# Attention results in the rotating FFN banks, last output tile in three parts, and a new planned order, in a fused attention and maxout-FFN kernel

## The chip, the cores and the metric

One core of one Trainium2 chip. The metric is the device time of one execution in microseconds (us). Most executions of a kernel agree within 0.3%; only runs in the fast state are compared, unless it is said otherwise. The profile's span (first to last instruction) is some 1.8 us shorter than the time.

## The reference

```python
# q, k, v: (4, 8, 768, 64) fp32; n_global 8, n_local 96; w1, w2, w3: (512, 768); w_out: (768, 512)
scores = q @ k.T / sqrt(64) - slope[h] * dist          # ALiBi-like bias
keep   = (key < 8) | (0 <= row - key < 96)              # first 8 keys, and a window of 96
a      = softmax(where(keep, scores, -1e9))
x      = (a @ v), heads joined                          # 3072 tokens x 512
h      = max(x @ w1, x @ w2, x @ w3)
out    = h @ w_out                                      # 3072 x 512, fp32
```

The 3072 tokens are 24 tiles of 128. A tile attends to itself and the tile before it. The FFN runs on seven chunks of 4, 2, 2, 4, 4, 4, 4 tiles.

## The kernel before

All instructions are emitted from one list, the planned order. A unit such as `S12.0.0` is a letter (what), a tile or chunk, and choices (head group, engine). The letters that matter: `S` scores and exp, `M` mask, `A` results times v with normalisation, `T` transpose of a result tile (`.4`: by DMA), `X`, `x` transpose of q and k, `F c.f.j` FFN unit of chunk c, slice f, weight j, `O` output unit, `w g.j` load of FFN weight j (its first 256 columns for g 0, the other 512 for g 1), `W g.j` cast of the third number g of its 768 columns, `E` the last chunk's output. Where a last digit names an engine, 0 is ScalarE, 1 VectorE and 2 GpSimd. Each engine runs its share of the list strictly in order.

```python
xb_pool  = tile_pool(name="xb",  bufs=3)       # attention result of a tile, bf16
ost_pool = tile_pool(name="ost", bufs=4)       # output staging
psS = tile_pool(name="psS", bufs=1, space=PSUM)  # tags sp0, sp1: two banks each
psH = tile_pool(name="psH", bufs=3, space=PSUM)  # tag h: three banks in rotation
psT = tile_pool(name="psT", bufs=1, space=PSUM)  # tag tp: one bank
# ... cut ...
def u_A(T, g):                                  # results times v
    op = psS.tile([128, 4, 65], FP32, name="op", tag=f"sp{g}")   # reuses its scores' banks
    # ... 8 matmuls ...
    nc.vector.reciprocal(rz, op[:, :, 64])
    nc.vector.tensor_tensor(out=x[:, 4*g:4*g+4], in0=op[:, :, 0:64], in1=rz..., op=mult)   # x is xb[T]

def u_XT(T, how):
    if how == 4:
        nc.sync.dma_start_transpose(out=xT[c][...], in_=xb[T]...)
    # ... cut: else on TensorE ...

def u_F1(c, f, j):                              # 4 matmuls into an h bank, then
    # j == 0: ACT copies it; j == 1, 2: VectorE takes the maximum with what is there

def f2_out(po, c, tt, copy, cols=slice(0, DM)):
    ost = ost_pool.tile(list(po.shape), FP32, name="ost", tag="ost")
    copy(ost, po)
    nc.sync.dma_start(out=out[T * 128:(T + 1) * 128, cols], in_=ost)

def u_E():                                      # last chunk: tiles 0..2 as 512 columns, then
    for i, copy in enumerate((nc.scalar.copy, nc.vector.tensor_copy)):
        cols = slice(i * 256, (i + 1) * 256)    # tile 3 in two halves
        # ... 6 matmuls, copy, store ...
```

The softmax here doesn't subtract the row's maximum and nothing guards it: scores larger than these inputs give would overflow.

## Time and profile before

| | before |
|---|---|
| median of 6 runs, us | 182.34 (182.04 to 182.61) |
| span of the profiled run, us | 180.0 |
| TensorE, VectorE, ScalarE busy | 93%, 68%, 60% |
| first FFN matmul, end of the last matmul, us | 24.98, 176.7 (its start plus its 0.11; the chain, with modelled ends, has 176.88) |

A page of the profile gives busy time per engine, then 40 slices of the span with tenths of busy time. The chain of work that ended last is followed back from the end, so an interval that stands in it is one that the next step waited for. PE is TensorE, PEld its weight loads, DVE VectorE, ACT ScalarE, POOL GpSimd, SPq and ACTq the DMA issues of SP and ACT. The lines themselves stand in the prediction.

### The profile page before, as it was taken

To read this page: it belongs to the slowest core of one execution; us is meant where nothing else is said; L and a number is where in the kernel's file an instruction comes from. 1 tells how busy PE (TensorE), PEld (TensorE's weight loads), DVE (VectorE), ACT (ScalarE), POOL (GpSimd) and SP (SyncE) were. 2 spreads that over 40 slices of the span, in tenths; PEclk is the share of its full clock that TensorE was granted. 3 is DMA by queue.
4 is the path that set the end of the run, shared out by engine and by line. 5 is a ranking of instruction groups with operands and counts; after the bars stand their busy time and mean duration, and the time that the engine had idled before them with its cause. 6 is when DMAs were issued, how large, how long until landed. Compare 5 with 4: busy or idle time off the path is not lost.

```text
span 180.0 us, 4007 instructions
## 1 busy us (share of the span) xinstructions
PE 167.2 (93%) x1534; PEld 94.5 (52%) x1534; DVE 122.0 (68%) x282; ACT 108.2 (60%) x164; POOL 35.0 (19%) x59
## 2 busy tenths in 40 slices
PE   0589979999999999999999999999999999999993
PEld 0345645555876787665455454454444545444442
DVE  3446477688796788769889878778877755144620
ACT  4987894966988867688555536374271753322122
POOL 6423524522052224201032001111004000000000
PEclk9999999999999999999999999999999999999999
DMA  5999999999988999999999999995998434610006
GB/s 147 275 267 284 263 350 306 355 254 261 298 178 198 274 213 234 103 232 265 187 185 249 160 232 226 257 140 136 252 198 166 99 93 146 204 58 0 4 0 233
DMA packets 91251, 35.91 MB, mean 200 GB/s; under 512 B 76000, under 2 KB 85984, under 8 KB 91232
## 3 DMA queue, kind: packets, MB, share of 16 engines
q1 hardware_dynamic: 91232, 35.66, 91.2%
q8 instruction: 12, 0.20, 0.5%
q14 instruction: 7, 0.06, 0.1%
HBM read 25.17 MB, written 6.29 MB: 175 GB/s over the span
## 4 chain that ended last, share of the span: by engine, by line
PE 78%; DMA 9%; SPq 9%; POOL 2%; issue 1%; DVE 0%; DVEq 0%; POOLq 0%
PE h L336 50%; PE po L351 16%; PE sp L260 5%; SPq L163 4%; DMA wst<-in_moe_w_dram 4%; SPq L148 3%; DMA qkT<-qkb 3%; PE op L297 3%; DMA xT<-xb 2%; PE op L300 2%; PE tp L238 1%; SPq L392 1%; PE xtp L324 1%; POOL w L402 1%; POOL qkb L185 1%
## 5 line engine op out<-in xcount | busy, mean ns | idle before, releaser
L336 PE MATMUL h<-xT,w 128*128 128x512 bf16 (+1 forms) x504 | 101.4, 349 | 0.8 <-DMA xT<-xb 0.4
L336 PEld LDWEIGHTS <-w 128*128 128x128 bf16 x504 | 46.3, 98 | 40.5 <-POOL w L402 0.9
L265 ACT ACTIVATE P<-sp 128x1024 bf16<-128x1024 f32 (+1 forms) x48 | 43.3, 950 | 22.5 <-PE sp L260 22.5
L351 PE MATMUL po<-wo,ht 128*128 128x512 bf16 (+1 forms) x150 | 33.9, 371 | 0.0
L343 DVE TENSOR_TENSOR h<-h,h 128x512 bf16<-128x512 bf16 (+1 forms) x42 | 25.2, 608 | 12.8 <-PE h L336 12.0
L341 ACT CAST h<-h 128x512 bf16<-128x512 f32 (+1 forms) x42 | 21.6, 531 | 18.5 <-PE h L336 18.0
L284 DVE TENSOR_TENSOR P<-P,wmask 128x1024 bf16<-128x1024 bf16 x34 | 23.4, 693 | 9.0 <-ACT P L265 8.9
L345 DVE TENSOR_TENSOR ht<-h,h 128x512 bf16<-128x512 bf16 (+1 forms) x42 | 25.2, 608 | 3.3 <-PE h L336 2.6
L357 ACT COPY ost<-po 128x512 f32<-128x512 f32 (+1 forms) x21 | 12.0, 577 | 18.4 <-PE po L351 16.0
L351 PEld LDWEIGHTS <-ht 128*128 128x128 bf16 x150 | 14.0, 98 | 14.7
L307 DVE TENSOR_TENSOR xb<-op,rz 128x256 bf16<-128x256 f32 x48 | 20.4, 424 | 1.7
L260 PE MATMUL sp<-qkT 64*128 64x128 bf16 x352 | 15.1, 220 | 1.1 <-DVE qkT L221 0.9
L297 PEld LDWEIGHTS <-P 128*128 128x128 bf16 x192 | 13.7, 99 | 4.3 <-ACT P L265 1.2
L260 PEld LDWEIGHTS <-qkT 64*128 64x128 bf16 x352 | 9.9, 94 | 11.3 <-issue 6.6
L297 PE MATMUL op<-va,P 128*128 128x65 bf16 x160 | 14.0, 193 | 0.9 <-ACT P L265 0.8
L306 DVE RECIPROCAL rz<-op 128x4 f32<-128x4 f32 x48 | 8.5, 178 | 9.2 <-PE op L300 5.8
L218 PE MATMUL tpp<-identb,qkp 128*128 128x128 bf16 x64 | 6.2, 254 | 6.6 <-DVE qkp L170 6.6
L300 PEld LDWEIGHTS <-P 128*128 128x128 bf16 x160 | 10.8, 97 | 1.5
L300 PE MATMUL op<-va,P 128*128 128x65 bf16 x128 | 11.2, 193 | 0.0
L176 POOL CAST va<-rawv 128x512 bf16<-128x512 f32 x9 | 5.8, 644 | 17.2 <-PE h L336 9.4
L185 POOL CAST qkb<-raw 128x1024 bf16<-128x1024 f32 x5 | 5.2, 1038 | 19.1 <-issue 13.6
L202 POOL COPY va<-vaf 8x260 int32<-8x260 int32 x10 | 4.4, 440 | 22.5 <-PE op L300 22.5
(68 smaller groups left out, 116.0 us busy)
## 6 DMA issues: line engine op xcount, KB each, us to landing
rawv<-in_v_dram SPq DMA_DIRECT2D x24, 256.0 KB, 5.5
out_dram<-ost SPq DMA_DIRECT2D x23, 256.0 KB, 3.1
raw<-in_q_dram SPq DMA_DIRECT2D x16, 256.0 KB, 5.3
raw<-in_k_dram SPq DMA_DIRECT2D x16, 256.0 KB, 5.0
wst<-in_moe_w_dram SPq DMA_DIRECT2D x3, 1024.0 KB, 9.9
rawp<-in_q_dram SPq DMA_DIRECT2D x4, 512.0 KB, 6.6
rawp<-in_k_dram SPq DMA_DIRECT2D x4, 512.0 KB, 6.5
wst<-in_moe_w_dram SPq DMA_DIRECT2D x3, 512.0 KB, 6.6
```

The source lines that it names most:

```text
L260: nc.tensor.matmul(sp[:, hh, j2, ds], qT(T - ds, 1)[hsl, jp], qT(T, 0)[hsl, jp], start=not how, stop=True, skip_group_check=True)
L265: nc.scalar.activation(P[:, :, 0:n], sp.rearrange("p a b d n -> p (a b) d n")[:, :, 0:n], AF.Exp, bias=0.0, scale=scale)
L284: nc.vector.tensor_mul(P, P, wmask[:, g, :, 0:2])
L297: nc.tensor.matmul(o, P[:, i, 0], heads(va[T])[:, h], start=True, stop=(t == 0), skip_group_check=True)
L300: nc.tensor.matmul(o, P[:, i, 1], heads(va[T - 1])[:, h], start=False, stop=True, skip_group_check=True)
L307: nc.vector.tensor_tensor(out=x[:, 4 * g:4 * g + 4], in0=op[:, :, 0:64], in1=rz[:, :, None].to_broadcast([128, 4, D]), op=ALU.mult)
L336: nc.tensor.matmul(ps, w123[f // 2][:, dm, j, (f % 2) * 128:(f % 2) * 128 + 128], xT[c][:, dm], start=(dm == 0), stop=(dm == 3))
L341: nc.scalar.copy(h01, ps)
L343: nc.vector.tensor_max(h01s[c, f], h01s[c, f], ps)
L345: nc.vector.tensor_max(ht[c][:, f], h01s[c, f], ps)
L351: nc.tensor.matmul(po, ht[c][:, f, tt * 128:(tt + 1) * 128], wo[:, f, cols], start=(f == 0), stop=(f == NF - 1))
L357: copy(ost, po)
```

## The change

The intent is to free the score banks earlier, shorten the end, and use both in a better order.

```diff
-    def u_A(T, g):
+    def u_A(T, g, how):
-        op = psS.tile([128, 4, 65], FP32, name="op", tag=f"sp{g}")
+        pool, tag = (psH, "h") if how else (psS, f"sp{g}")
+        op = pool.tile([128, 4, 65], FP32, name="op", tag=tag)
 ...
-    def f2_out(po, c, tt, copy, cols=slice(0, DM)):
+    def f2_out(po, c, tt, copy, cols=slice(0, DM), dma=nc.sync):
-        nc.sync.dma_start(out=out[T * 128:(T + 1) * 128, cols], in_=ost)
+        dma.dma_start(out=out[T * 128:(T + 1) * 128, cols], in_=ost)
 ...
-        for i, copy in enumerate((nc.scalar.copy, nc.vector.tensor_copy)):
-            cols = slice(i * 256, (i + 1) * 256)
+        for lo, hi, copy, dma in ((0, 256, nc.scalar.copy, nc.sync), (256, 384, nc.vector.tensor_copy, nc.sync),
+                                  (384, 512, nc.scalar.copy, nc.scalar)):
 ... (the planned order: all 506 units in a new order, many casts and copies on another engine; 41 of 48 A units with how = 1; excerpt)
-    ... M5.1 W1.0.2 F0.2.0 F0.3.0 F0.4.0 c3.0.2 x3.0.3 ...
+    ... W1.0.0 l3.1 W2.0.0 w1.1 v4 F0.0.2 S5.0.0 S5.1.0 M5.0 M5.1 F0.2.0 F0.3.0 F0.1.2 F0.4.0 ...
-    ... C20.0.3 v20 C18.1.1 O3.0.1 S18.0.0 ... T17.4 F4.2.2 O3.2.0 A19.0 A19.1 T18.4 ...
+    ... O3.0.0 O3.1.1 C20.1.0 S19.0.0 X21.4 S19.1.0 A18.1.1 M19.0 O3.2.0 O3.3.0 X22.4 T17.4 A19.0.1 G19.2 T18.4 ...
```

More of the change, by code (lines that the diff above doesn't have):

```diff
@@ L25 @@
 SCHEDULE = """
-    K0 K1 K2 K3 K4 K5 K6 K7 l1.0 v0 v1 B0.1 B1.0 c0.0.1 c0.1.1 B2.1 B3.1 B4.2 B5.0 B6.0 x0.0.2 x0.1.3
-    c1.0.0 S0.0.1 B7.2 S0.1.1 M0.0 M0.1 C0.1.2 C1.1.0 A0.0 G0.0 x1.0.2 A0.1 S1.0.1 S1.1.1 l1.1 M1.0 G1.1
-    l2.0 c1.1.2 l2.1 M1.1 c2.0.1 v2 w0.1 v3 v4 x1.1.2 w0.0 A1.0 A1.1 c2.1.2 V1.2 x2.0.1 C2.1.2 S2.0.1
-    S2.1.1 G2.2 C3.1.2 T0.1 M2.0 M2.1 A2.0 x2.1.2 A2.1 V2.1 S3.0.1 S3.1.1 T1.0 T2.0 G3.2 W0.1.2 M3.0
-    M3.1 A3.0 W0.0.2 A3.1 S4.0.0 T3.1 w0.2 S4.1.0 M4.0 M4.1 G4.1 C4.1.1 W0.2.0 F0.0.0 V3.1 F0.1.0 F0.0.1
@@ L31 @@
-    w1.0 F0.1.1 A4.0 A4.1 F0.0.2 F0.1.2 W2.0.0 S5.0.0 M5.0 l3.0 S5.1.0 M5.1 W1.0.2 F0.2.0 F0.3.0 F0.4.0
-    c3.0.2 x3.0.3 v5 C5.1.2 T4.0 w1.1 V4.2 A5.0 W2.1.0 l3.1 F0.5.0 W1.1.2 c3.1.1 F0.2.1 F0.3.1 x3.1.2
-    A5.1 F0.4.1 w1.2 W1.2.0 F0.5.1 S6.0.0 S6.1.0 v6 C6.1.0 v7 C7.1.0 T5.0 M6.0 M6.1 W2.2.2 F0.2.2 F0.3.2
-    F0.4.2 F0.5.2 F1.0.0 F1.1.0 A6.0 F1.2.0 A6.1 L8 F1.0.1 F1.1.1 o2 Q2.0 G6.0 S7.0.0 o0 S7.1.0 F1.2.1
-    G7.0 F1.0.2 F1.1.2 T6.0 M7.0 M7.1 F1.3.0 F1.4.0 F1.5.0 A7.0 C8.0.2 X8.3 A7.1 Q0.0 v8 o1 L9 L10
@@ L36 @@
-    F1.3.1 F1.4.1 F1.5.1 S8.0.0 S8.1.0 v9 V7.2 G8.1 L11 C8.1.0 M8.0 Q1.2 O0.0.0 v10 v11 C9.0.2 M8.1
-    O0.1.0 A8.0 X9.0 A8.1 V8.2 O0.2.0 C10.0.0 T7.1 F1.2.2 F1.3.2 F1.4.2 S9.0.0 M9.0 S9.1.0 M9.1 C9.1.2
-    L12 L13 L14 G9.1 X10.1 O0.3.0 F2.0.0 F2.0.1 A9.0 F2.1.0 A9.1 F1.5.2 F2.0.2 v12 F2.2.0 T8.1 S10.0.0
-    S10.1.0 F2.1.1 F2.2.1 F2.3.0 C11.0.2 X11.0 M10.0 F2.4.0 M10.1 F2.1.2 F2.5.0 V9.2 G10.1 C10.1.2 A10.0
-    A10.1 V10.2 C11.1.2 C12.0.2 X12.4 C12.1.2 C13.0.0 X13.4 F2.2.2 T9.1 F2.3.1 F2.3.2 L15 S11.0.0 M11.0
@@ L41 @@
-    S11.1.0 v13 v14 v15 v16 M11.1 O1.0.0 F2.4.1 A11.0 O1.1.0 T10.0 A11.1 F2.5.1 F2.4.2 T11.0 S12.0.0
-    M12.0 S12.1.0 G12.1 M12.1 F2.5.2 C14.0.0 F3.0.0 F3.1.0 A12.0 A12.1 F3.0.1 C15.0.1 X14.3 S13.0.0
-    S13.1.0 G13.1 M13.0 M13.1 X15.4 O2.0.0 C13.1.0 F3.0.2 C14.1.1 C15.1.2 F3.2.0 A13.0 A13.1 C16.1.1
-    F3.1.1 F3.2.1 S14.0.0 S14.1.0 G14.2 V13.1 T12.4 M14.0 M14.1 F3.3.0 F3.1.2 F3.4.0 L16 T13.4 A14.0
-    A14.1 F3.3.1 F3.4.1 S15.0.0 S15.1.0 C16.0.3 L17 L18 M15.0 M15.1 F3.5.0 T14.4 O2.1.0 G15.2 V14.2
@@ L46 @@
-    A15.0 X16.1 A15.1 V15.2 T15.4 F3.2.2 F3.3.2 C17.0.0 F3.4.2 S16.0.0 M16.0 S16.1.0 L19 F3.5.1 F3.5.2
-    X17.4 v17 A16.0 M16.1 F4.0.0 F4.1.0 C18.0.3 F4.0.1 F4.1.1 G16.2 v18 C17.1.0 A16.1 F4.0.2 X18.4
-    F4.1.2 S17.0.0 S17.1.0 L20 T16.4 F4.2.0 F4.3.0 F4.4.0 V16.1 C19.0.1 M17.0 X19.4 L21 M17.1 v19 A17.0
-    A17.1 C20.0.3 v20 C18.1.1 O3.0.1 S18.0.0 M18.0 S18.1.0 O3.1.0 C19.1.2 M18.1 F4.2.1 A18.0 A18.1
-    F4.3.1 F4.4.1 G18.1 X20.4 S19.0.0 S19.1.0 C20.1.0 F4.5.0 M19.0 M19.1 T17.4 F4.2.2 O3.2.0 A19.0 A19.1
@@ L51 @@
-    T18.4 F4.5.1 T19.4 L22 V19.2 G19.2 C21.0.3 O3.3.1 S20.0.0 M20.0 S20.1.0 G20.1 X21.4 v21 L23 v22
-    F4.3.2 v23 F4.4.2 A20.0 F4.5.2 M20.1 F5.0.0 F5.0.1 F5.1.0 A20.1 C22.0.1 C23.0.2 F5.0.2 F5.1.1
-    S21.0.0 S21.1.0 F5.2.0 M21.0 M21.1 F5.3.0 F5.2.1 F5.3.1 C21.1.0 C22.1.2 F5.1.2 X22.4 O4.0.0 V20.1
-    A21.0 T20.4 A21.1 F5.2.2 F5.3.2 G21.0 S22.0.0 S22.1.0 M22.0 M22.1 F5.4.0 F5.4.1 X23.4 G22.1 C23.1.0
-    V21.2 A22.0 F5.5.0 A22.1 O4.1.0 F5.5.1 S23.0.0 M23.0 S23.1.0 F5.4.2 M23.1 T21.4 T22.4 O4.2.0 F5.5.2
@@ L56 @@
-    O4.3.0 V22.1 A23.0 A23.1 T23.4 O5.0.0 O5.1.0 O5.2.0 O5.3.1 F6.0.0 F6.1.0 F6.2.0 F6.0.1 F6.1.1 F6.2.1
-    F6.3.0 F6.0.2 F6.1.2 F6.2.2 F6.4.0 F6.5.0 F6.3.1 F6.4.1 F6.3.2 F6.4.2 F6.5.1 F6.5.2 E
+    c0.0.2 K0 B0.0 l1.0 K1 l1.1 l2.0 K2 K3 K4 B1.1 B2.0 B3.1 B4.0 B5.0 B6.0 x0.0.0 B7.0 c0.1.2 c1.0.2
+    c1.1.1 x0.1.2 x1.0.3 c2.0.1 S0.0.0 S0.1.1 G0.1 S1.0.0 v0 x1.1.1 v1 M0.0 K5 K6 K7 M0.1 M1.0 l2.1
+    C0.1.2 S1.1.1 M1.1 G1.2 S2.0.1 M2.0 v2 C1.1.1 v3 w0.0 w0.1 w0.2 A0.0.1 A0.1.1 S2.1.0 G2.2 c2.1.2
@@ new lines @@
+    x2.0.0 A1.0.1 S3.0.1 A1.1.1 C2.1.2 V1.2 M2.1 T0.0 M3.0 S3.1.1 C3.1.1 A2.0.1 A2.1.1 T1.0 V2.2 A3.0.0
+    x2.1.0 M3.1 T2.0 A3.1.0 T3.1 W0.0.2 G3.2 S4.0.0 S4.1.0 W0.2.1 M4.0 F0.0.0 F0.1.0 w1.0 V3.1 M4.1 l3.0
+    W0.1.2 F0.0.1 F0.1.1 G4.2 W1.0.0 l3.1 W2.0.0 w1.1 v4 F0.0.2 S5.0.0 S5.1.0 M5.0 M5.1 F0.2.0 F0.3.0
+    F0.1.2 F0.4.0 w1.2 c3.0.2 c3.1.2 x3.0.3 x3.1.0 W1.2.2 W1.1.1 W2.1.0 C4.1.1 F0.5.0 S6.0.1 S6.1.0 G6.2
+    W2.2.0 F0.2.1 F0.3.1 v5 A4.0.1 F0.4.1 F0.5.1 A4.1.1 o2 S7.0.0 V4.2 L8 S7.1.0 F0.2.2 T4.0 C5.1.2
@@ new lines @@
+    A5.0.1 A5.1.1 F0.3.2 F0.4.2 T5.0 F0.5.2 F1.0.0 v6 F1.0.1 C8.0.2 X8.3 M6.0 F1.1.0 F1.2.0 F1.3.0 M6.1
+    M7.0 C6.1.0 G7.0 L9 F1.1.1 F1.2.1 o0 F1.0.2 M7.1 F1.4.0 Q2.2 C9.0.2 X9.3 F1.3.1 F1.4.1 S8.0.0 S8.1.0
+    G8.1 L10 C10.0.2 A6.0.1 v7 F1.1.2 F1.2.2 o1 F1.5.0 F1.5.1 F1.3.2 F1.4.2 L11 v8 Q0.0 v9 C7.1.2 X10.0
+    A6.1.1 L12 S9.0.0 S9.1.0 A7.0.1 A7.1.1 Q1.2 F1.5.2 M8.0 C11.0.1 X11.4 L13 T6.0 v10 V7.2 O0.0.0
+    C8.1.0 O0.1.0 G9.1 S10.0.0 v11 M8.1 M9.0 S10.1.0 A8.0.1 A8.1.1 T7.1 T8.4 O0.2.0 O0.3.0 F2.0.0 M9.1
@@ new lines @@
+    M10.0 V8.2 F2.1.0 M10.1 C9.1.1 C12.0.1 F2.0.1 F2.0.2 G10.0 S11.0.0 S11.1.0 F2.1.1 A9.0.1 X12.1
+    F2.2.0 F2.3.0 A9.1.1 F2.1.2 C10.1.0 C13.0.2 X13.3 F2.4.0 S12.0.0 L14 V9.2 S12.1.0 A10.0.1 M11.0
+    M11.1 v12 v13 A10.1.1 V10.2 C11.1.1 O1.0.0 T9.0 M12.0 G12.0 O1.1.0 F2.2.1 F2.3.1 F2.5.0 v14 L15
+    C12.1.2 C13.1.2 T10.0 A11.0.1 A11.1.1 v15 v16 S13.0.0 S13.1.0 F2.2.2 F2.3.2 F2.4.1 F2.5.1 T11.1
+    G13.0 L16 F2.4.2 C14.0.0 C15.0.2 F2.5.2 A12.0.1 M12.1 M13.0 M13.1 X14.0 F3.0.0 F3.1.0 A12.1.1 F3.0.1
@@ new lines @@
+    F3.1.1 F3.2.0 A13.0.0 A13.1.0 F3.0.2 X15.4 F3.1.2 C14.1.1 C15.1.1 S14.0.0 S14.1.0 G14.2 V13.1 M14.0
+    M14.1 F3.3.0 C16.1.2 F3.4.0 C16.0.0 T12.4 T13.4 O2.0.1 A14.0.1 F3.2.1 F3.2.2 A14.1.1 S15.0.0 M15.0
+    S15.1.0 F3.5.0 X16.4 v17 T14.0 G15.0 V14.1 M15.1 L17 F3.3.1 F3.3.2 L18 v18 v19 F3.4.1 C17.1.0 F3.4.2
+    A15.0.1 A15.1.1 S16.0.0 M16.0 S16.1.0 G16.2 C17.0.1 F3.5.1 F3.5.2 T15.0 X17.4 O2.1.1 M16.1 C18.0.0
+    V15.2 F4.0.0 F4.1.0 A16.0.0 L19 F4.0.1 F4.1.1 A16.1.1 C18.1.2 S17.0.0 S17.1.0 M17.0 F4.0.2 F4.2.0
@@ new lines @@
+    F4.2.1 F4.1.2 M17.1 F4.3.0 C19.0.2 F4.3.1 F4.2.2 F4.3.2 L20 C20.0.0 V16.2 X18.4 S18.0.0 M18.0 T16.4
+    S18.1.0 L21 L22 F4.4.0 A17.0.1 F4.5.0 A17.1.1 F4.4.1 F4.5.1 F4.4.2 F4.5.2 G18.0 v20 C21.0.2 C22.0.3
+    C19.1.2 X19.4 X20.4 M18.1 A18.0.1 v21 O3.0.0 O3.1.1 C20.1.0 S19.0.0 X21.4 S19.1.0 A18.1.1 M19.0
+    O3.2.0 O3.3.0 X22.4 T17.4 A19.0.1 G19.2 T18.4 S20.0.0 S20.1.0 M19.1 M20.0 O4.0.1 A19.1.1 M20.1
+    C21.1.2 T19.4 L23 G20.2 S21.0.0 M21.0 v22 S21.1.0 V19.2 O4.1.0 G21.2 A20.0.1 O4.2.1 v23 S22.0.0
@@ new lines @@
+    S22.1.0 A20.1.1 O4.3.0 V20.1 A21.0.1 M21.1 M22.0 M22.1 G22.2 F5.0.0 F5.1.0 F5.0.1 F5.2.0 C23.0.1
+    F5.3.0 A21.1.1 F5.1.1 F5.0.2 C22.1.0 V21.2 A22.0.1 F5.2.1 X23.4 F5.1.2 T20.4 T21.4 F5.2.2 S23.0.0
+    S23.1.0 C23.1.1 A22.1.1 F5.4.0 M23.0 V22.2 M23.1 F5.5.0 A23.0.0 F5.3.1 A23.1.0 T22.4 T23.4 F5.4.1
+    F5.5.1 F5.3.2 F5.4.2 F5.5.2 F6.0.0 F6.0.1 O5.0.1 O5.1.0 F6.0.2 F6.1.0 F6.2.0 F6.3.0 F6.4.0 F6.1.1
+    F6.2.1 F6.3.1 F6.4.1 F6.1.2 F6.2.2 F6.3.2 O5.2.1 O5.3.1 F6.4.2 F6.5.0 F6.5.1 F6.5.2 E
@@ L376, in u_E @@
             f2_out(po, last, tt, nc.scalar.copy)
-        for i, copy in enumerate((nc.scalar.copy, nc.vector.tensor_copy)):
-            cols = slice(i * 256, (i + 1) * 256)
-            po = psH.tile([128, 256], FP32, name="po", tag="h")
-            f2_mm(po, last, n - 1, range(NF), cols)
-            f2_out(po, last, n - 1, copy, cols)
+        for lo, hi, copy, dma in ((0, 256, nc.scalar.copy, nc.sync), (256, 384, nc.vector.tensor_copy, nc.sync),
+                                  (384, 512, nc.scalar.copy, nc.scalar)):
+            po = psH.tile([128, hi - lo], FP32, name="po", tag="h")
+            f2_mm(po, last, n - 1, range(NF), slice(lo, hi))
+            f2_out(po, last, n - 1, copy, slice(lo, hi), dma)
     wsrc = [moe_w1, moe_w2, moe_w3]
```

## The prediction

> **What bounds the kernel now.** I read the page first. Section 1 and the tenths line of section 2 show TensorE (PE) busy for 93% of a span of 180.0 us, idle only in the first slices and the last (a slice is 4.5 us):
>
> ```profile
> span 180.0 us, 4007 instructions
> PE 167.2 (93%) x1534; PEld 94.5 (52%) x1534; DVE 122.0 (68%) x282; ACT 108.2 (60%) x164; POOL 35.0 (19%) x59
> PE   0589979999999999999999999999999999999993
> DVE  3446477688796788769889878778877755144620
> DMA  5999999999988999999999999995998434610006
> ```
>
> Busy PE is not proof of a dense PE, so I took a table of stretches (columns: stretch, length, then busy time and number of instructions per engine, clock, DMA share, GB/s) and the chain of work that ended last in order of time (start, length, what):
>
> ```profile
> 0.00:5.84 5.84, 0.00 (x0) 0.00 (x0) 2.23 (x14) 3.59 (x8) 4.12 (x14) 1.00 0.68 180
> 5.84:24.98 19.14, 16.03 (x208) 9.93 (x208) 10.49 (x27) 17.08 (x26) 7.70 (x11) 1.00 1.18 277
> 24.98:76.00 51.02, 51.02 (x550) 34.52 (x551) 40.24 (x95) 38.78 (x60) 15.11 (x19) 1.00 1.04 251
> 103.00:150.00 47.00, 47.00 (x386) 23.15 (x384) 36.01 (x79) 23.94 (x36) 4.50 (x8) 1.00 0.90 179
> ```
>
> ```profile
> 16.89 6.95 DMA wst<-in_moe_w_dram
> 23.83 0.05 issue
> 23.89 1.05 POOL w L402
> 24.94 0.05 issue
> 24.98 3.63 PE h L336 x16
> ...
> 97.12 4.38 DMA xT<-xb
> ...
> 150.95 5.18 PE po L351 x24
> 156.13 15.54 PE h L336 x72
> 171.67 5.21 PE po L351 x30
> 176.88 0.04 DVEq L357
> ...
> 176.96 0.42 DVE ost L357
> ```
>
> So there are three regions. **Head** (to 24.98): loads, casts, exp and masks of the first tiles; it ends when the first FFN weight has landed and been cast. **Body** (24.98 to 176.88): PE back to back; starts that came late behind a wait (read in the timeline) add up to about 1.1 us, the largest 0.6 at 101.5 (a transposing DMA of xb) and 0.4 at 76.5 (one of qkb). **Tail** (3.1 us): last copy, last store. The list of waits says the same: after the head the matmuls wait 0.4 us for xT by DMA and 0.2 for qkT by DMA, and nothing larger.
>
> **What the Trainium skill says.** "TensorE: Matmul & The Clock Gate", section "Wait — 56ns, not 53.3ns?": back-to-back 512-column matmuls start 215.7 ns apart when warm. The trace agrees: 24 in 5.18 us is 216 ns. "PSUM — Partial Sum Buffer", Specifications: 8 banks of 2 KiB per partition, a matmul output at most one. By the pools all are taken: sp0 and sp1 two each, three for h, one for tp. No spare bank exists, so results times v must borrow. "DMA: Bandwidth & Descriptors", "Issuing engines are not separate DMA queues": a second issuing engine saves only issue time; here an output store's issue takes 0.33 us. "ScalarE: Activation LUTs", "What ACT_TABLE_LOAD costs": an ACTIVATE with immediates takes 186 ns + 0.833 ns per column; the 512-column copies of this trace took 577 ns on average (formula 613), so 128 columns are estimated at 0.29 us.
>
> **The change part by part.**
> (1) 41 of the 48 results-times-v units write into a rotating h bank instead of the sp bank that their scores used. Removed: scores of the next tile waiting for VectorE to read op; they now wait only for the exp. Work stays the same. As the body has almost no waits, this itself can save at most part of 1.1 us there; it helps the head, where scores, exp, mask and results follow closely. Added: the h rotation of three is used 197 times instead of 159. A bank is reusable about 0.85 us after results times v (gap 0.2, RECIPROCAL 0.18, TENSOR_TENSOR 0.42), 0.8 to 0.9 after an FFN unit. I laid both orders out by PE work and looked three users back: before one place falls short, by 0.1 us; after four, 0.6 us together, if the readers are free.
> (2) PE work. Units: FFN 4x0.216=0.864 (two-tile chunks 4x0.109), output 6x0.216=1.296, results 8x0.03=0.24, scores 8x0.0275+0.12=0.33, bias 0.53 more, transposes 0.056 each. Without the final unit the old order sums to 157.6 and the new to 156.75: two fewer biased scores (8 to 6, and one moved to a half-size tile), one more xT transposed on PE (12 to 11 by DMA). The 0.85 saved lies in the head, where PE is not the limit.
> (3) Head. Weights w0 are loaded earlier: 4.5 MB (units of 1024 KB) ahead of and including the first weight instead of 5.25, so that it is no longer last to arrive. Walking the new order by hand: ten masks and biases on ACT at 0.44 end near 8.1, then two qkT copies (1.0 each), exp 0.97 each; the second tile pair's qkT is on VectorE at 15.1, exp of tile 3 ends at 21.3, its results are scaled at 22.8, transposed and copied at 23.6. The first FFN matmul comes at about **23.9** instead of 24.98.
> (4) What that is worth is decided later: the FFN's third weight w1.2 is the last to land. In the old trace casts began at 34.62 (w1.1, 8.5 MB of loads) and 39.11 (w1.2, 10.0 MB), and the first matmul with the latter at 40.69. In the new order w1.1 still has 8.5 MB, w1.2 9.75, as one v tile moved behind. 1.5 MB took 4.49 us, so w1.2 should land 0.75 us earlier, 38.35, and with POOL's cast of 1.04 be usable at **39.4**. PE gets there at 39.4 to 39.9: after 35.3 (w1.1 at 34.6 plus a VectorE cast of 0.69) come 4 FFN units, two results and two half scores, 4.6 us. From there remain 130.5 us of PE work after and 130.0 before, plus 5.2 of the final unit. Check on the old kernel: 40.69+130.0+5.2=175.9, and measured 176.88; the missing 1.0 is its waits. New: 39.4+130.5+5.2=175.1, plus waits.
> (5) Waits of the new body, the term I know least. Shortfalls of the h rotation 0.6; the last chunk's xT: between tile 23's results and its FFN stand five FFN units (4.3 us) where four outputs (5.2 us) stood, against about 1.3 on VectorE and 2.4 to 3.6 of DMA, about 0.2; VectorE, given more copies (output copies on it 3 to 8, v casts 4 to 8), is loaded to about 104% of PE time in one 10 us stretch near chunk 1, about 0.4. Sum **1.2**, end of PE 176.3, or 0.6 before the old.
> (6) Tail. 12 matmuls of 256 columns become 6 of 256 and 12 of 128: same PE time. The last copy goes from VectorE 0.42 to ACT about 0.29, which is reached some 0.1 later; the last store halves. SP was not behind (five issues of 0.33 to 0.41), so a second queue saves little. Gain **0.2**.
> Sum: -0.6 - 0.2 = -0.8, so 182.3 becomes **181.5 us**.
>
> **Rivals.** *Rotation becomes the bound*: each borrowed bank waits for VectorE, 68% busy on average and 77 to 79% in the long stretches of the body; if it is 0.15 us late at 20 places, waits are 3 us more and the time is 184. For it: VectorE is in order and its masks (0.69) stand before these reads. Against: the new order puts 3 to 15 us of PE work between scores and results where 2 to 6 stood. *Free PE*: looser spacing takes away all body waits and loads arrive sooner; then PE ends at 175.1 or slightly earlier, and the time is 180 to 180.3. Against a larger gain: the matmuls themselves do not shrink, and DMA is at full share until 45 us. *Head gain wholly lost*: the weights decide, landing as before; PE ends where it did, 182.1 to 182.5. *Transposing DMAs*: 11+10 instead of 12+10, in other places; if two come late, as at 76 and 101 before, +1.
>
> **Range and chances.** The head's arrival is uncertain by 0.7 us, waits by about +2 and -1, tail by 0.2: 180.0 to 183.6 eight times in ten. Faster by over 2% means under 178.7, below even the wait-free sum by 1.4, so 0.04. Slower means over 186.0, 4 us of new waits, 0.04.
>
> **What would show it.** In the new profile: the first h matmul near 23.9; the cast of w1.2 near 38.4 and the chain passing through it; PE 9 in all middle slices, with waits of matmuls for VectorE's xb (the rotation) summing to about 0.6; the last chunk's h waiting 0.2 for DMA xT; tail from last matmul near 2.9. It is wrong if loads with another order run at another speed (head), or if op in the h banks shows waits of several us.

## The result, and the profile after

The changed kernel takes **182.45 us** (median of 6 runs, 182.29 to 182.83), the kernel before 182.34. A ratio is the mean time of one kernel's fast runs over the mean of the other's from the same rounds, so it is not quite the ratio of the medians: here 1.0009, 95% interval 0.9996 to 1.0022. The forecast gain of 0.8 us did not appear.

From the page of the changed kernel:

```profile
span 180.7 us, 3999 instructions
PE 166.1 (92%) x1520; PEld 96.2 (53%) x1540; DVE 125.9 (70%) x279; ACT 105.6 (58%) x164; POOL 35.1 (19%) x64
PE   0489898999999999999999999999989999999992
```

Two of PE's middle slices are now an 8 where before all were 9: the seventh (27 to 32 us) and the thirtieth (131 to 136 us). (20 matmul records of 1540 are missing from this trace; the weight loads are complete, and times of units below are taken from them.) The chain of waits of the changed kernel, in order of time (start, length, what):

```profile
17.43 9.78 DMA wst<-in_moe_w_dram
27.23 0.90 ACT w L404
...
29.13 1.16 ACT P L266 x2
...
30.95 0.59 ACT h L343
...
31.59 0.81 PE h L338 x3
...
127.07 6.65 DMA xT<-xb x2
...
174.96 0.60 ACT ost L359
...
175.58 2.25 DMA out_dram<-ost
...
177.92 0.27 ACT ost L359
```

Three things stand in it that the old chain did not have. Near 30 us PE waits for an h bank that ACT had no time to copy, having two weight casts and two exps ahead of it. At 127 us stands a transposing DMA of attention results. At the end ACT's last copy stands behind an output store of 2.25 us; ACT was idle for 0.91 of them.

To see where time came and went, I took the start of chosen units and added the PE work still to come by the unit costs of the prediction (150.7 us at the first FFN unit before, 151.2 after). A number that rises from one row to the next is a wait in between; changes of up to 0.2 can come from the rounded unit costs. "Before again" is one more profile of the same kernel, taken with the last round (experiment 9; a single run).

| projected end of PE, from | before | before again | changed |
|---|---|---|---|
| first FFN unit (starts 24.98, 25.52, 23.26) | 175.7 | 176.2 | 174.5 |
| first unit with weight w1.2 | 175.7 | 176.2 | 175.3 |
| chunk 4 | 176.7 | 177.0 | 175.7 |
| chunk 5 | 176.5 | 176.9 | 177.1 |
| chunk 6 | 176.5 | 176.9 | 176.9 |
| measured end of the last matmul | 176.7 | 177.1 | 177.1 |
| span | 180.0 | 180.4 | 180.7 |

The head gives 1.2 us, more than forecast. 0.8 is lost again before w1.2, the old order's two waits for transposing DMAs (76 and 101 us) are saved, 1.4 is lost between chunks 4 and 5 (1.0 in the profiles of experiments 1 and 4, see there), and from the end of the last matmul to the end of the span it takes 3.6 us instead of 3.3. The first profile of before was a quick one (181.75 us against its median of 182.34), which goes with the 0.4 between the two spans of this kernel.

### The profile page after: what moved, and what is told of

The parts are those of the page before. It is cut to its first block, busy times and chain, and to the rows that moved or that the text cites. A ratio compares the mean times of both kernels' runs of the same rounds, so it can differ in the third digit from the quotient of the medians.

```text
span 180.7 us, 3999 instructions
## 1 busy us (share of the span) xinstructions
PE 166.1 (92%) x1520; PEld 96.2 (53%) x1540; DVE 125.9 (70%) x279; ACT 105.6 (58%) x164; POOL 35.1 (19%) x64
## 4 chain that ended last, share of the span: by engine, by line
PE 71%; DMA 10%; SPq 10%; ACT 4%; issue 2%; DVE 1%; ACTq 0%; DVEq 0%
PE h L338 46%; PE po L353 13%; DMA wst<-in_moe_w_dram 5%; PE sp L261 4%; SPq L149 4%; DMA xT<-xb 4%; SPq L164 3%; PE op L299 3%; PE op L302 2%; SPq L394 1%; DMA out_dram<-ost 1%; ACT P L266 1%; PE tp L239 1%; PE xtp L326 1%; ACT ost L359 1%
## 5 line engine op out<-in xcount | busy, mean ns | idle before, releaser
L338 PE MATMUL h<-xT,w 128*128 128x512 bf16 (+1 forms) x489 | 99.8, 348 | 1.5 <-ACT h L343 0.5
L338 PEld LDWEIGHTS <-w 128*128 128x128 bf16 x504 | 46.8, 98 | 41.0 <-issue 1.2
L353 PE MATMUL po<-wo,ht 128*128 128x512 bf16 (+2 forms) x151 | 33.2, 362 | 1.0 <-DVE xb L309 0.7
L285 DVE TENSOR_TENSOR P<-P,wmask 128x1024 bf16<-128x1024 bf16 x36 | 25.8, 737 | 3.0 <-ACT P L266 2.6
L359 ACT COPY ost<-po 128x512 f32<-128x512 f32 (+2 forms) x17 | 9.3, 556 | 16.1 <-PE po L353 13.0
L299 PE MATMUL op<-va,P 128*128 128x65 bf16 x160 | 14.3, 194 | 0.0
L186 POOL CAST qkb<-raw 128x1024 bf16<-128x1024 f32 x7 | 7.4, 1054 | 26.6 <-DMA raw<-in_k_dram 26.6
L302 PE MATMUL op<-va,P 128*128 128x65 bf16 x128 | 11.4, 193 | 0.1
L359 DVE COPY ost<-po 128x512 f32<-128x512 f32 (+1 forms) x9 | 5.8, 644 | 7.6 <-PE po L353 7.6
```

The lines of the kernel that those rows point to most:

```text
L285: nc.vector.tensor_mul(P, P, wmask[:, g, :, 0:2])
L299: nc.tensor.matmul(o, P[:, i, 0], heads(va[T])[:, h], start=True, stop=(t == 0), skip_group_check=True)
L302: nc.tensor.matmul(o, P[:, i, 1], heads(va[T - 1])[:, h], start=False, stop=True, skip_group_check=True)
L338: nc.tensor.matmul(ps, w123[f // 2][:, dm, j, (f % 2) * 128:(f % 2) * 128 + 128], xT[c][:, dm], start=(dm == 0), stop=(dm == 3))
L353: nc.tensor.matmul(po, ht[c][:, f, tt * 128:(tt + 1) * 128], wo[:, f, cols], start=(f == 0), stop=(f == NF - 1))
```

## The experiments

Twelve runs, all with correct results (experiment 9 is the kernel before itself). "Before" in the table is the kernel before in the same rounds.

| | edit | median us | ratio to before, 95% |
|---|---|---|---|
| (changed) | | 182.45 | 1.0009 (0.9996 to 1.0022) |
| 1 | changed, six staging tiles | 182.23 | 0.9990 (0.9967 to 1.0013) |
| 2 | before, three parts | 182.75 | 1.0018 (0.9998 to 1.0039) |
| 3 | before, three parts, six staging tiles | 182.21 | 0.9989 (0.9969 to 1.0009) |
| 4 | changed, five xb tiles | 182.56 | 1.0006 (0.9978 to 1.0034) |
| 5 | changed, two transposes earlier | 181.80 | 0.9957 (0.9940 to 0.9974) |
| 6 | changed, one cast on POOL | 181.46 | 0.9950 (0.9927 to 0.9973) |
| 7 | changed, no rotation | 205.99 and 206.32 fast | 1.1291 (1.1261 to 1.1321) |
| 8 | 1, 5 and 6 together | 180.80 | 0.9901 (0.9881 to 0.9920) |
| 9 | before, one look | 182.16 | - |
| 10 | before, with rotation | 189.66 | 1.0384 (1.0362 to 1.0407) |
| 11 | 8 with two parts | 181.10 | 0.9910 (0.9891 to 0.9930) |
| 12 | changed, stores by ACT | 183.73 (one of six runs slow; fast ones 183.65) | 1.0055 (1.0028 to 1.0082) |

### The tail: experiments 1, 2, 3 and 11

Theory A: three parts make six output pieces in the last unit, the pool of staging tiles has four, so the sixth piece must wait until the second piece's store has landed.

```diff
# experiment 1 (on the changed kernel) and 3 (on the kernel before, with the three-part loop put in)
-    ost_pool = tile_pool(name="ost", bufs=4)
+    ost_pool = tile_pool(name="ost", bufs=6)
# experiment 2: the kernel before with the three-part loop of the change, bufs=4
# experiment 11: experiment 8 with
-        for lo, hi, copy, dma in ((0, 256, scalar.copy, sync), (256, 384, vector.tensor_copy, sync), (384, 512, scalar.copy, scalar)):
+        for lo, hi, copy, dma in ((0, 256, scalar.copy, sync), (256, 512, vector.tensor_copy, sync)):
```

> The changed kernel with six output staging tiles instead of four, nothing else. Theory A (the last copy of the changed kernel waits until the store of the second 256 KB tile has landed, because six output pieces share four staging tiles): ACT's last copy starts within 0.3 us of the last matmul (177.1) instead of at 177.92, the wait of ACT for the store (0.9 us) is gone, tail 2.8 us instead of 3.6, time 181.7 +-0.2. Rival (the tail is set by the store traffic itself or by the store queued on ScalarE): the copy moves forward but the last landing does not, time 182.3 to 182.5.

> The kernel before with only the three-part output of the last tile (four staging tiles, old order, no rotation). Theory A: the sixth piece must wait for a staging tile here too, so the time rises by 0.5 to 0.7 us over the kernel before (182.8 to 183.0). Rival: three parts with a second queue shorten the tail by 0.2 (182.1), as predicted.

> As the run before, with six staging tiles. Theory A: the loss is gone and the part does what it was meant to: 0.1 to 0.3 us under the kernel before (182.0 to 182.2). Rival: no difference from the run with four staging tiles.

> The combined kernel (six staging tiles, early transposes of tiles 17 and 18, cast on POOL) with the last tile's columns again in two parts on SP. Theory (three parts with a second queue gain nothing even with staging tiles enough: last landing 2.4 to 2.5 us after the end of the last matmul either way): 180.6 to 181.0, within 0.2 of the combined kernel. Rival: 0.2 to 0.4 slower than the combined kernel.

The copies on ACT at the end, as the timeline shows them (start, length, engine, what, and in brackets the idle time before it with what ended it). The changed kernel, then the kernel before with three parts and six staging tiles (experiment 3):

```profile
177.92 0.27 ACT L359 COPY ost<-po 128x128 f32<-128x128 f32 x1 [0.91 <-DMA out_dram<-ost]
```

```profile
177.31 0.27 ACT L357 COPY ost<-po 128x128 f32<-128x128 f32 x1 [0.25 <-PE po L351]
```

With four staging tiles the last copy waits for a store, with six for the matmul. From the end of the last matmul to the end of the span, in the profiles:

| | two parts | three parts, four tiles | three parts, six tiles |
|---|---|---|---|
| old order | 3.28, 3.27 (before, twice) | 3.70 (2) | 3.31 (3) |
| new order | 3.26 (11) | 3.56 (changed) | 3.29 (1), 3.28 (8) |

So the wait is shown, in both orders: it costs 0.3 to 0.4 us. The other four profiles of the new order with four tiles (4, 5, 6, 12) have 3.52 to 3.55 as well. The forward move of ACT's copy did not bring the 0.5 to 0.75 of time that I expected of experiments 1 and 2: its store goes out 0.6 us earlier (2 against 3), but lands after 1.9 to 2.0 us instead of 1.6. That it then queues with the stores before it is likely, and not shown. And with staging tiles enough, three parts and a second queue are worth nothing that these profiles resolve: the copy is 0.15 us shorter, but the last store still lands 2.4 to 2.5 us after the last matmul. The times are too rough to decide it: experiment 2 against 3 differs by 0.5 us in the median with intervals that overlap a little, and 8 and 11 overlap.

### The stretch from 127 to 134 us: experiments 4, 5 and 12

The change has PE waiting twice there. In the list of waits (us in all, times, longest), the changed kernel has, for PE and for DVE:

```profile
PE po L353 <- DVE xb L309: 0.7, 1, 0.7
```

```profile
DVE xb L309 <- DMA xT<-xb: 2.2, 1, 2.2
```

Theory B: SP issues its DMAs in order. The transpose of tile 17 stands in the list behind four output stores, and a store is issued when its copy is done; so the transpose goes out late, its xb tile (three exist) cannot be overwritten with tile 20's results, VectorE stands, an h bank is not read, and PE stands. DMA queue of SP in the changed kernel, then in experiment 5:

```profile
120.37 1.76 SPq L360 DMA_DIRECT2D out_dram<-ost  x2
122.22 1.30 SPq L228 DMA_TRANSPOSE qkT<-qkb  x1
123.83 1.54 SPq L360 DMA_DIRECT2D out_dram<-ost  x2
125.48 1.54 SPq L228 DMA_TRANSPOSE qkT<-qkb  x1
127.07 3.52 SPq L317 DMA_TRANSPOSE xT<-xb  x2
...
131.32 1.22 SPq L317 DMA_TRANSPOSE xT<-xb  x1
```

```profile
119.39 1.47 SPq L321 DMA_TRANSPOSE xT<-xb  x1
120.96 1.18 SPq L364 DMA_DIRECT2D out_dram<-ost  x2
...
128.43 1.21 SPq L321 DMA_TRANSPOSE xT<-xb  x1
```

Chunk 5 consists of tiles 16 to 19, so its first unit needs tile 19's transpose, the last line of each: in the changed kernel it lands at 133.72 and PE starts that unit at 133.76.

```diff
# experiment 4
-    xb_pool = tile_pool(name="xb", bufs=3)
+    xb_pool = tile_pool(name="xb", bufs=5)
# experiment 5: planned order only
-    O3.0.0 O3.1.1 C20.1.0 S19.0.0 X21.4 S19.1.0 A18.1.1 M19.0 O3.2.0 O3.3.0 X22.4 T17.4 A19.0.1 G19.2 T18.4
+    T17.4 O3.0.0 O3.1.1 C20.1.0 S19.0.0 X21.4 S19.1.0 A18.1.1 M19.0 T18.4 O3.2.0 O3.3.0 X22.4 A19.0.1 G19.2
# experiment 12: in the ordinary output unit
-        f2_out(po, c, tt, copies[how])
+        f2_out(po, c, tt, copies[how], dma=nc.sync if how else nc.scalar)
```

> The changed kernel with five xb tiles instead of three. Theory B (around 129 us VectorE waits 2.2 us to write xb of tile 20, since tile 17's xb is still to be read by a transposing DMA; VectorE being in order, an h bank is not read and PE stands 0.85 us): that wait and PE's 0.7 us wait before an output unit vanish, time 0.6 to 0.9 lower, 181.6 to 181.8; the later wait for tile 19's xT (0.5) may stay. Rival (VectorE is simply overloaded there): PE's wait only moves, less than 0.2 us gained.

> The changed kernel with the transposing DMAs of tiles 17 and 18 moved in the planned order ahead of chunk 3's output units, so that on SP they do not stand behind output stores that wait for their copies. Theory B (head-of-line on SP: in the changed kernel the one for tile 17 was issued at 127.07, 2 us after a store whose copy only ended at 125.0, though its xb was ready near 118.5): VectorE's wait for xb (2.2 us), PE's 0.85 us stand before an output unit and the 0.5 us before the first FFN unit of chunk 5 all go; PE's last matmul 1.0 to 1.4 us earlier relative to the first FFN matmul, time 181.0 to 181.5 (if the last output copy still waits for its staging tile). Rival (transposing DMAs are slow there because of other DMA traffic): issue moves earlier, landing and waits stay, time as the changed kernel.

> The changed kernel with the output stores whose copy is ACT's own issued by ACT instead of SP, planned order untouched. Theory B (on SP the transposing DMA of tile 17 stands behind stores that wait for their copy): it is issued 1.5 to 2.5 us earlier than 127.07, VectorE's wait for xb shrinks from 2.2 to under 0.7 and PE's waits between 127 and 134 us from 1.4 to under 0.6; against it stand some 12 issues of 0.37 on ACT, which is not the bound: time 181.4 to 182.0. Rival: ACT's issues make its h copies late, PE waits elsewhere, 182.4 or more.

Experiment 4 missed its time. VectorE's wait for xb is gone and with it PE's stand before the output unit, but the wait of the first unit of chunk 5 for its transposed inputs grew from 0.5 to 1.0 us by the projected ends (0.3 to 0.7 in the list of waits, at its weight load): the transposes were as late as before, and a spare buffer only let PE run into them. Of 1.4 us lost, 1.0 stayed. Nor are the other 0.4 the buffers' doing: experiment 1, with three xb tiles and the same order, loses 1.0 there too. SP took 2.17 us to issue tile 18's transpose in the changed kernel's profile, and 1.22 in those of experiments 1, 4 and 6, so that tile 19's went out sooner. SP's queue in experiment 1:

```profile
127.49 2.58 SPq L317 DMA_TRANSPOSE xT<-xb  x2
```

Experiment 5 agrees with theory B. Tile 17's transpose goes out 7.7 us earlier, VectorE never waits for xb, and the projected end rises only from 175.7 (chunk 4) to 176.0 (chunk 5), where the changed kernel went to 177.1. From the first FFN matmul to the last it is 1.2 us shorter, as expected. The time is 0.95 us below the changed kernel by the ratios (0.0052 of 182.4), at the edge of what I expected; the median, 181.80, lies 0.3 above it. The rival, slow transposes in any place, is refuted: from issue to landing the three took 3.6 us in the median, where the changed kernel had 3.3, but they landed earlier. The edit does not tell the stores from the rest of the queue, for tile 17's transpose also moves ahead of two of q and k, which took SP 1.30 and 1.54 us to issue. Its xb was complete at 115.5 (not 118.5, as the expectation has it), so that even here it went out late.

Experiment 12 attacks the same cause from another side, and missed. Counted from tile 19's scores, which start 1.3 us later in this run, tile 17's transpose is issued 2.1 us earlier than in the changed kernel, and VectorE's wait for xb is gone, as theory B has it. So the stores whose copy is ACT's are 2.1 of the 7.7 us; the store of VectorE's copy and the two transposes of q and k still stand ahead. But the kernel is slower by 0.8 us, and between chunks 4 and 5 as much is lost as before (1.5 by the projected ends): for chunk 5 PE still waits for a transpose, and two of the three took SP 2.1 to 2.2 us to issue. From its waits of PE:

```profile
PE h L338 <- ACT h L343: 0.8, 2, 0.5
PE h L338 <- DMA xT<-xb: 0.7, 1, 0.7
```

The rival that I named, ACT made late by its own issues, is not shown as the cause. Of the 0.8 in the first line 0.5 is the wait at 31.6 us that the changed kernel has too; the other 0.3, at 65 us, fits the rival, as does a wait for an exp at 129 us (0.3). But one of 0.4, for VectorE, stands at 52.6 us, before ACT has issued its first store (58.8). What made this kernel slower stays open in part.

### The stretch from 28 to 35 us: experiment 6

```diff
-    W2.0.0      # cast of the third 256 columns of the first FFN weight on ACT
+    W2.0.2      # the same cast on POOL
```

> The changed kernel with one cast of the FFN weight w1.0 (third 256 columns) moved from ACT to POOL. Theory C (around 28 to 32 us an h bank waits for ACT, which does two weight casts and two exps before the h copy): PE's wait near 31.6 us (0.65) goes and the first FFN unit with w1.1 starts 0.5 to 0.8 earlier; what then remains depends on w1.1 (cast near 34.3 to 35.0) and w1.2 (cast done at 38.6): time 181.7 to 182.1. Rival (loads of weights bound that stretch, as the prediction said): the wait moves to the unit with w1.1 or w1.2, time within 0.2 of the changed kernel.

The chain of waits of experiment 6 in that stretch:

```profile
27.55 1.05 ACT w L404
28.60 0.05 issue
28.65 3.41 PE h L338 x15
```

(Both orders have this cast on ACT; the new one also put `W1.0` there, which was POOL's before.) One cast instead of two, and PE runs on: the projected end goes from 174.7 (first FFN unit) to 175.0 (w1.2), where the changed kernel went from 174.5 to 175.3. Theory C holds, and its rival, that the arrival of weights bounds this stretch, does not: in the changed kernel the casts of w1.2 began at 37.6 us and were done at 38.6, one microsecond before PE's first unit with it at 39.6. The time fell by 1.1 us against the changed kernel (ratios 0.9950 and 1.0009, the first with an interval of 0.4 us to each side), where this stretch gives 0.6. Another 0.4 lies further on, though nothing was changed there: between chunks 4 and 5 the projected end rises by 0.9 instead of 1.4, about as in experiments 1 and 4. The two transposes took SP 2.57 us to issue here and 3.52 in the changed kernel; why is not settled, and I don't count this part for the cast.

### What the rotation is for: experiments 7 and 10

```diff
# experiment 7, changed kernel: A4.0.1 A4.1.1 ... -> A4.0.0 A4.1.0 ... (all 41)
# experiment 10, kernel before: the new u_A, and A4.0 A4.1 ... -> A4.0.1 A4.1.1 ... (all 48)
```

> The changed kernel with all results times v back in their sp banks, same new order. If the rotation is what allows the new order: scores then wait for VectorE's reads of results that the new order puts late, PE gets waits of 0.3 us and more at many score units, time 183 to 186. Rival (the rotation hardly matters, the order alone does it): time 182.2 to 182.8.

> The kernel before with all results times v in the rotating h banks, old order. Theory: in the old order results come only 2 to 5 us of PE work after their scores and the sp banks are free in time, so the rotation takes away nothing and adds users of the h banks in an order not made for it: PE waits 0.2 to 0.5 us at a dozen units, time 183 to 186. Rival (the rotation alone is a gain that the new order spoils): 180.5 to 181.8.

Both parts alone are bad: the new order without the rotation takes 206 us (its two fast runs; the other four, the profiled one among them, slow), the old order with it 189.7. In the profile of experiment 7, which is a slow one, PE waits

```profile
PE op L303 <- ACT P L270: 12.7, 13, 1.8
PE sp L265 <- DVE xb L313: 5.7, 8, 1.1
```

for exps, and for score banks that VectorE has not read. The new order puts up to 18 us of PE work between a tile's scores and its results, and by then the next tile's scores need the bank. Experiment 10 spends its 7 us in many small waits, most of them for h banks (its profile is that of its slowest run, 191.73). I had expected at most 186 for each; the size surprised me, the direction did not. The new order and the rotation are one change.

### All repairs together: experiment 8, and the kernel before again: experiment 9

> The changed kernel with six staging tiles, tiles 17 and 18 transposed early, and that weight cast on POOL. If the three losses are separate and add up: 0.4 (tail) + 1.2 + 0.5 less, 180.2 to 180.6, under both kernels by about 1%. Rival (losses stand in for each other, another wait takes over): 181.3 to 182.

> The kernel before, profiled once more, to see how far its head varies from run to run: the first profile had the first FFN matmul at 24.98, two variants of it with the same head on another chip 25.5. Expected 24.9 to 25.6, last matmul about 151.6 us after it, and waits near 76 and 101 us of 0.4 to 0.7 as before. If instead the body varies by over 0.3, comparisons of single profiles are weaker than I take them.

The combined kernel takes 180.8 us, 0.99% under the kernel before and 1.1% under the changed one. It is 0.2 to 0.6 above what I hoped for. Its projected ends are 174.8 at the first FFN unit, 175.0 at w1.2, 175.5 at chunk 4, 175.7 at chunk 5 and 175.5 at chunk 6, so nearly nothing is lost on the way. Its PE waits after the head are

```profile
PE op L303 <- ACT va L181: 0.3, 1, 0.3
PE po L357 <- issue: 0.2, 1, 0.2
```

Against the changed kernel, experiments 1, 5 and 6 save 0.0019, 0.0052 and 0.0059 in ratio, 0.0130 in sum; together they save 0.0108. The difference, 0.4 us, is no larger than the intervals, so the losses were separate as far as this shows. Experiment 9 shows how far one kernel's profiles differ: the first FFN matmul at 25.52 instead of 24.98, as its weight landed later, and from there to the end of the last matmul 151.6 us against 151.7. Experiments 2 and 3, with the same order, also have 151.6. So a single profile of this order is good to about 0.1 us for the body and tail, and to 0.5 for the head; the new order's body differs by 0.3 between the changed kernel and experiment 1, where nothing but the staging tiles was changed.

## Why the prediction was wrong

- **Head (step 3): right in direction, short in size.** 23.9 us forecast for the first FFN matmul, 23.26 measured (23.3 to 24.1 in the other profiles of the new order with the rotation).
- **Weights decide (step 4): right number by luck, wrong reason.** I had PE at the first w1.2 unit at 39.4 to 39.9 with the weight usable at 39.4; it came at 39.6. But the weight was usable at 38.6. What held PE was ACT near 30 us, where two casts of 1.0 us and two exps stand ahead of an h copy; experiment 6 shows it. My layout of the h banks tested each place as if its reader were free, and said so; ACT was not.
- **Waits of the new body (step 5): the first term that was mis-sized.** I put 1.2 us: 0.6 for the rotation in four places, 0.2 at the last chunk, 0.4 for VectorE's load near chunk 1. After w1.2 the projected ends rise by 1.6 to chunk 6. About 0.3 lies near chunk 1, and none at the last chunk; 1.4 lies between 127 and 134 us (0.9 to 1.0 in the profiles of experiments 1, 4 and 6), where I had nothing. The step looked at PE's order and at the work of the readers, and never laid out SP's order. The Trainium skill states the piece I needed, "DMA: Bandwidth & Descriptors", in a note of the section "Anatomy of one DMA — SWDGE (gpsimd) path": waits on semaphores are made by the issuing sequencer before dispatch, the DMA engines only consume their queues. The trace agrees for SP: the transpose of tile 17 went out at 127.07, behind stores whose copies were late and two other transposes, and 7.7 us earlier when moved ahead of them.
- **The tail (step 6): the second term, with the wrong sign.** I forecast a gain of 0.2. It is a loss of 0.3 (3.56 against 3.28 us), because I counted instructions and issues and not the staging tiles, six pieces over four. Without that wait the gain is nil, not 0.2.
- **The rivals.** Of those I gave, the rotation as the bound was worth 184; in the combined kernel, rotation and all, the projected end rises by only 0.9 us in the whole body. "Transposing DMAs come late" was there with +1, for the right resource, and I gave it no share in the sum. "Free PE", 180.0 to 180.3, is near the combined kernel's 180.8. One figure against the rotation as the bound was off: the new order puts 1.6 to 18.5 us of PE work between a tile's scores and its results, not 3 to 15.
- **The sum.** Forecast 181.5, measured 182.45. From profile to profile the miss is 1.5. Waits and the point at w1.2 cost 0.6 to 0.8 more than forecast and the tail 0.5; some 0.2 more comes from a mixed reading, since the forecast end of PE, built from starts of units, was set against the chain's modelled 176.88 and not against 176.7. Against it the profile of before was 0.6 quicker than the kernel's usual run (181.75 against 182.34), so that I started from an end that was too early.
- **Small slips that change nothing.** 8x0.0275+0.12 is 0.34 and not 0.33. The 577 ns for a 512-column copy is the mean of a group with one copy of 256 columns; alone, those of 512 took 587. And that a matmul's output takes at most one bank stands in "The four PSUM rules" of the page that I named, not in its Specifications.

## What to carry to other kernels

When an order is replanned on a bounded engine, lay out every in-order queue that feeds it, the DMA-issuing one too: a transfer that frees a buffer must not stand behind stores that wait for late copies. Count the staging buffers when the last output is split into more pieces (here four for six pieces made a wait, and six did not); it gained nothing here, where the last store's landing, not the copy, ends the kernel. A spare buffer in front of a late transfer moved the wait, an earlier issue removed it. And before a difference of a few tenths in one profile is credited to an edit, look for it in a run without that edit.

## What the Trainium skill lacked or had wrong

- "DMA: Bandwidth & Descriptors", section "Latency and other measured facts", gives the DMA transposes of one kernel an effective bandwidth of 261 GB/s, and some 350 to 400 for a contiguous case. Here a transpose of 128x512 bf16 (128 KB) between SBUF tiles took 2.4 to 6.0 us from issue to landing, 3.0 in the median, which is at best some 55 GB/s, and mostly 1.2, at times up to 2.4 us of SP's time to issue; a plain store's issue took 0.33. The page has no time from issue to landing for a single small one.
- No page that I read says what a queue in order does to buffers elsewhere: stores waiting for their copies, and other transposes, held a transpose, and through one xb tile VectorE for 2.2 us and PE for 0.85.
- "ScalarE: Activation LUTs", section "What ACT_TABLE_LOAD costs": an ACTIVATE's 186 ns + 0.833 ns per column would be 293, 399 and 613 ns for 128, 256 and 512 columns. Copies out of PSUM measured 265, 372 and 585 ns, about 28 less in each case; casts of 512 columns out of SBUF measured 620 to 625, some 10 more. The page does not tell the two sources apart.
- "DMA: Bandwidth & Descriptors", "Issuing engines are not separate DMA queues", is borne out: with staging tiles enough, three parts with the last store on the ACT queue brought nothing at the end (3.28 to 3.31 us against 3.26 to 3.28). It does not mention the other side, that issues take their place in the engine's own work (0.34 us each on ACT, experiment 12).
